# Splitting half of one weight row into a 126-partition and a 2-partition transfer, in a decode kernel that streams 309 MB

## The chip, the core and the metric

The kernel runs on one core of one Trainium2 chip. The metric is the device time of that core in microseconds (us), from one execution of the program; three runs of the kernel before gave 720.33, 720.45 and 720.57 us, median 720.45. The profiled execution was a fourth run of 720.52 us. Its span, from the first to the last profiled instruction, is 718.7 us; the remaining 1.8 us lie around the span.

## The reference

Two branches read the same two tokens `x` (2 x 576) and are mixed by a gate:

```
g = sigmoid(sum(x * gate_w))
q = x @ wq                                   # 32 heads of 128
scores = q . k_cache / sqrt(128)             # k_cache: 2 x 32 x 4096 x 128
a = (softmax(scores) @ v_cache) @ wo         # wo: 4096 x 576
b = gelu(x @ w1 + b1) @ w2 + b2              # w2: 4608 x 576
out = g * a + (1 - g) * b                    # 2 x 1 x 576
```

All of it is float32. Nearly all bytes are the two caches, 128 MiB each; `wq`, `w1`, `w2` and `wo` are 9 to 11 MB each.

## The kernel before, in words

One large SBUF tile, `ring`, has three slots of 64 KiB per partition. Projections come first: `wq` and `w1` are loaded into the ring, q and the hidden layer are computed, and the small inputs (`x`, `gate_w`, `b1`, `b2`) come by ACT's queue. Then 16 passes follow, each with four heads of one batch element: K goes into slots 0 and 1 in turn, V into slot 2. VectorE multiplies K by q (line 521), POOL and VectorE sum over the head dimension (lines 525 to 528), ScalarE takes the exponentials (549), and TensorE multiplies by V (564) and collects into bank 1 (581).

The last stage loads `w2` and `wo` into slots as they come free, on SP's queue. The rows are named by number: `wo` is seen as 128 partitions with 32 rows of 576 columns each, so "row r" of `wo` is a 128 x 576 matrix with one 2304-byte piece in each partition. `w2` has 36 such rows. The transfers stand in this order:

| transfer | rows | bytes per partition | slot |
|---|---|---|---|
| w2 | 0-13, 14-27 | 32256 each | 2 |
| w2 | 28-35 | 18432 | 1 |
| wo | 0-8 | 20736 | 1 |
| wo | 9-15 | 16128 | 1 |
| wo | 16-22 | 16128 | 0 |
| wo | 23-26, 27-29, 30 | 9216, 6912, 2304 | 0 |
| wo | 31 in three parts | 1152, 576, 576 | 0 |

Slot 0 holds the last V until `attend` of the last pass has read it; the transfers into slot 0 therefore wait for TensorE.

TensorE then goes through the rows in the same order: `acc_mm` (line 428) makes two products of 288 columns for each row of `w2` and for rows 0 to 22 of `wo`, into bank 0; rows 23 to 31 go as four products of 144 columns into bank 7 (`part`, line 699). After row 26 the half-sums of bank 0 are folded in (`folds`, 706). Row 31 is taken in the three parts in which it arrives. The result is copied by VectorE and ScalarE (724) and stored by SP (727).

Order and waits are made by a small class, `Flow`. Each `op` names what it reads (`r`), writes (`w`) and shares in writing (`a`); `plan` turns these into semaphore waits, and each transfer has a semaphore of its own (`d1`, `d2`, ...), so that a consumer waits for the whole transfer. Within an engine the order is that of the program's text. `load_rows` (607) issues one transfer for a run of rows and notes for each row where it lies and by which name it is waited for; `row` (648) looks that up for TensorE.

Of the kernel before, what the change touches and what calls it, by code (L numbers as in the profile page):

```python
# [12 lines left out]
P = 128  # L13
# [120 lines left out]
def kernel(  # L134
# [16 lines left out]
    D = x.shape[-1]  # L151
# [20 lines left out]
    DO = D // NC  # L172
# [5 lines left out]
    SLOT = R * DH  # L178
# [14 lines left out]
    ring = rp.tile([P, SLOTS * SLOT], F32, name="ring")  # L193
# [16 lines left out]
    hg = cp.tile([P, NF, B], F32, name="hg")  # L210
# [3 lines left out]
    def temp(n, parts=P):  # L214
        t = ring[:parts, used["t"]:used["t"] + n]
        used["t"] += n
        assert used["t"] <= SLOTS * SLOT
        return t
# [12 lines left out]
    with tc.tile_critical() as section:  # L231
        f = Flow(nc, {"first": first})
# [10 lines left out]
        def pe(fn, r=(), w=(), a=(), loop=None):  # L243
            return f.op("pe", fn, r, w, a, loop=loop)

        def load(out_, in_, r=(), w=(), e="sp", key=None, a=()):
            f.seq = getattr(f, "seq", 0) + 1
            key = key or f"d{f.seq}"
            at = f.at[e]
            return f.op(e, lambda: at.dma_start(out_, in_), r, w, a, dma=key)  # L250
# [3 lines left out]
        def mm(o, lhsT, rhs, start, stop):  # L254
            return ten.matmul(o, lhsT, rhs, start=start, stop=stop, skip_group_check=True)  # L255


        at = 0
        wts = {}
        for name, w in (("wq", wq), ("w1", w1)):  # L260
            n = w.shape[1]
# [22 lines left out]
        for b in range(B):  # L284
# [20 lines left out]
            r=["ident"], w=["pick"],  # L305
# [73 lines left out]
        def gather():  # L379
# [11 lines left out]
            r=["ident"], w=["mine"],  # L391
# [4 lines left out]
            r=["ident"], w=["row4"],  # L396
# [7 lines left out]
        for g in range(N // NQ):  # L404
            u = g * NQ
            t = temp(NQ * DH, NO).rearrange("p (u d) -> p u d", u=NQ)
# [12 lines left out]
                r=[f"bank{b}"], w=[f"q{g}"],  # L419
# [4 lines left out]
        def half_mm(lhsT, rhs, k, s, start=False):  # L424
            o = 64 * (k % 2) + 32 * s
            return mm(acc[o:o + lhsT.shape[-1]], lhsT, rhs, start, False)

        def acc_mm(lhsT, rhs, k, start=False):
            for s in range(NS):
                i = half_mm(lhsT, rhs[:, s * DS:(s + 1) * DS], k, s, start)  # L430
            return i
# [153 lines left out]
        for i in range(N):  # L585
# [10 lines left out]
            s = i % 2  # L596
# [7 lines left out]
        srcs = {"w2": w2.rearrange("(p r) n -> p (r n)", r=NF), "wo": wo.rearrange("(p r) n -> p (r n)", r=32)}  # L604
        rows = {}

        def load_rows(o, w, a, z, part=None):
            lo, hi = part or (a * D, z * D)
            name = f"{w}:{lo}"
            load(ring[:, o:o + hi - lo], srcs[w][:, lo:hi], w=[name], r=[f"free{o // SLOT}"])  # L610
            for r in range(a, z):
                first, end = max(r * D, lo), min((r + 1) * D, hi)
                rows.setdefault((w, r), []).append((first - r * D, end - r * D, o + first - lo, name))
            return o + hi - lo
# [9 lines left out]

        release(2)
        o = load_rows(2 * SLOT, "w2", 0, 14)
        o = load_rows(o, "w2", 14, 28)
        release(1)
        o = load_rows(SLOT, "w2", 28, NF)
        o = load_rows(o, "wo", 0, 9)  # L630
        o = load_rows(o, "wo", 9, 16)
        assert o <= 2 * SLOT
        attend(k, "slot0")
        release(0)
        o = 0
        for a, z in ((16, 23), (23, 27), (27, 30), (30, 31)):
            o = load_rows(o, "wo", a, z)
        for a, z in ((0, DS), (DS, DS + DO), (DS + DO, D)):
            o = load_rows(o, "wo", 31, 32, (31 * D + a, 31 * D + z))
        used["e"] = o  # L640

        def late(n, parts=P):
            t = ring[:parts, used["e"]:used["e"] + n]
            used["e"] += n
            assert used["e"] <= SLOT
            return t

        def row(w, r, lo=0, hi=D):
            for a, z, o, name in rows[w, r]:
                if a <= lo and hi <= z:  # L650
                    return ring[:, o + lo - a:o + hi - a], name

        keep(k)
        combine(k)
# [8 lines left out]
        oP = late(B * 32).rearrange("p (b c) -> p b c", b=B)  # L663
# [7 lines left out]
            r=["bank1", "free0"], w=["osum"],  # L671
# [14 lines left out]
        dve(lambda: vec.tensor_copy(oP.rearrange("p b c -> p (b c)"), opps), r=["bank5"], w=["oP"])  # L686

        for r in range(NF):
            t, name = row("w2", r)
            pe(lambda t=t, r=r: acc_mm(hg[:, r], t, r), r=["hg", name], a=["bank0"])  # L690
        for r in range(FOLD):
            t, name = row("wo", r)
            pe(lambda t=t, r=r: acc_mm(oP[:, :, r], t, r), r=["oP", name], a=["bank0"])

        sums2 = late(DS)
        act(lambda: sca.copy(sums2, acc), r=["bank0", "free0"], w=["sums2"])
        res = bank[7][:32 * (NC - 1) + B, :DO]

        def part(r, s):
            t, name = row("wo", r, s * DO, (s + 1) * DO)  # L700
            pe(
                lambda: mm(res[32 * s:32 * s + B], oP[:, :, r], t, r == FOLD, r == 31),
                r=["oP", name], a=[f"bank7"] if r < 31 else [f"bank7", f"res{s}"],
            )

        def folds():
# [5 lines left out]
        for r in range(FOLD, 31):  # L712
            for s in range(NC):
                part(r, s)
            if r == FOLD + 3:
                pe(folds, r=["fold", "sums2"], a=["bank7"])
        osb = late(D, B)
        for h in ((0, 1), (2,), (3,)):
            for s in h:
                part(31, s)  # L720
            for s in h:
                on, cpy = (dve, vec.tensor_copy) if s % 2 == 0 else (act, sca.copy)
                on(
                    lambda s=s, cpy=cpy: cpy(osb[:, s * DO:(s + 1) * DO], res[32 * s:32 * s + B]),  # L724
                    r=[f"res{s}", "free0"], w=[f"osb{s}"],
                )
# [35 lines left out]
```

## Time and profile before

| what | value |
|---|---|
| runs | 720.33, 720.45, 720.57 us |
| profiled execution | 720.52 us, span 718.7 us |
| moved by DMA | 308.70 MB, mean 430 GB/s |
| VectorE busy | 518.2 us (72%) |
| TensorE matmuls busy | 242.9 us (34%) |
| POOL busy, ScalarE busy | 144.2 us, 41.6 us |
| chain that ended last | DMA 56%, VectorE 38%, TensorE 4% |

The busy share of the 16 DMA engines stands at nine tenths or more in 39 of the 40 slices of the span. In short stretches that share comes out up to a tenth above or below what it is over a long one, and 1.00 is read as all 16 engines at work. A queue row of the page gives packets, not transfers: each partition's contiguous piece is a packet of its own, and completions are counted as packets too.

### The profile page before, as it was taken

Reading aid. Unit: us, or ns where it says so; the run is one execution under the profiler, and the core shown is the slowest. Engines: PE = TensorE matmul, PEld = TensorE weight load, DVE = VectorE, ACT = ScalarE, POOL = GpSimd, SP = SyncE. Lnnn points to the kernel's source line nnn. Section 1 sums busy time; section 2 is a strip of 40 time slices with the busy share of each in tenths; the row PEclk is TensorE's granted clock in tenths of the full one; section 3 lists DMA queues with packets and bytes.
Section 4 is the critical chain, followed back from the end, with each engine's and each line's share of the span. In section 5 each row is a group of like instructions: output and inputs, shape, how many; then the busy total and the mean of one; then the engine's idle time right before and its main releaser. Section 6 shows DMA issues by size and latency. Waiting matters only on the chain.

```text
span 718.7 us, 3902 instructions
## 1 busy us (share of the span) xinstructions
PE 242.9 (34%) x1659; PEld 69.3 (10%) x1659; DVE 518.2 (72%) x150; ACT 41.6 (6%) x157; POOL 144.2 (20%) x28
## 2 busy tenths in 40 slices
PE   0685005141514132140605060514123150506566
PEld 0221001010101000010101010101000010101122
DVE  0103999999969696969698896969696969798100
ACT  0020010101010101010101000010101010101000
POOL 1020133140404040211304040404030220304000
PEclk9977557575656657565657565656656565757888
DMA  9999999999999999999999999999999999999997
GB/s 411 413 420 453 419 456 416 453 419 434 434 427 445 423 452 423 445 423 430 441 427 445 423 452 423 445 423 423 449 423 449 423 449 423 441 427 427 422 429 319
DMA packets 7075, 308.70 MB, mean 430 GB/s; under 512 B 782, under 2 KB 1166, under 8 KB 1436
## 3 DMA queue, kind: packets, MB, share of 16 engines
q1 hardware_dynamic: 7044, 308.55, 99.3%
q8 instruction: 5, 0.08, 0.0%
q10 hardware_dynamic: 24, 0.05, 0.0%
q14 instruction: 2, 0.02, 0.0%
HBM read 308.59 MB, written 0.00 MB: 429 GB/s over the span
## 4 chain that ended last, share of the span: by engine, by line
DMA 56%; DVE 38%; PE 4%; POOL 0%; issue 0%; ACTq 0%; ACT 0%; POOLq 0%; DVEq 0%
DMA ring<-in_A_k_cache_dram 43%; DVE ring L521 22%; DVE st L526 11%; DMA ring<-in_A_v_cache_dram 6%; DVE st L528 5%; DMA ring<-in_A_wo_dram 4%; PE bank L255 4%; DMA ring<-in_gate_w_dram 3%; POOL ring L275 0%; PE bank L320 0%; DVE mxt L597 0%; DVE bs L538 0%; ACTq L250 0%; POOL ring L369 0%; DVE ring L313 0%
## 5 line engine op out<-in xcount | busy, mean ns | idle before, releaser
L521 DVE TENSOR_TENSOR ring<-ring,q_all 128x16384 f32<-128x16384 f32 x16 | 275.6, 17224 | 84.4 <-DMA ring<-in_A_k_cache_dram 84.4
L255 PE MATMUL bank<-ring,p_all 128*32 128x512 f32 x1024 | 148.4, 744 | 342.7 <-DMA ring<-in_A_v_cache_dram 342.7
L525 POOL TENSOR_TENSOR ring<-ring 128x3968 f32<-128x3968 f32 x16 | 137.9, 8622 | 473.1 <-DVE ring L521 473.1
L526 DVE TENSOR_REDUCE st<-ring 128x66 f32<-128x8448 f32 x16 | 143.2, 8953 | 0.5
L255 PEld LDWEIGHTS bank<-ring,p_all 128*32 128x32 f32 x1024 | 36.1, 133 | 460.4 <-DMA ring<-in_A_v_cache_dram 355.5
L528 DVE TENSOR_REDUCE st<-ring 128x62 f32<-128x3968 f32 x16 | 68.6, 4286 | 0.6
L549 ACT ACTIVATE p_all<-st,bs 32x128 f32<-32x128 f32 x64 | 25.5, 398 | 561.1 <-DVE bs L538 560.5
L255 PE MATMUL bank<-ring 128*32 128x384 f32 (+8 forms) x410 | 49.0, 538 | 10.7 <-DMA ring<-in_A_wo_dram 7.0
L255 PE MATMUL bank<-ident,mxt 128*128 128x128 f32 x32 | 9.6, 390 | 90.9 <-DVE mxt L597 90.9
L491 DVE TENSOR_TENSOR ring<-bank,ring 128x384 f32<-128x384 f32 x3 | 1.5, 553 | 33.3 <-PE bank L255 33.3
L255 PE MATMUL bank<-avs,now 128*64 128x512 f32 x32 | 24.1, 844 | 2.0 <-DVE avs L574 0.9
L724 DVE COPY ring<-bank 2x144 f32<-2x144 f32 x2 | 0.6, 300 | 32.7 <-PE bank L255 32.7
L574 DVE TENSOR_TENSOR avs<-bank,selr 128x512 f32<-128x512 f32 x16 | 10.9, 680 | 16.0 <-PE bank L255 16.0
L255 PEld LDWEIGHTS bank<-ring 128*32 128x32 f32 (+5 forms) x410 | 18.4, 124 | 40.7 <-issue 23.4
L255 PEld LDWEIGHTS bank<-ident,mxt 128*128 128x128 f32 x32 | 5.9, 232 | 105.2 <-DVE mxt L597 105.2
L313 DVE COPY ring<-ring 3x64 f32<-3x64 f32 x2 | 0.3, 183 | 19.1 <-DMA ring<-in_gate_w_dram 19.1
L549 ACT ACTIVATION_READ_ACCUMULATOR p_all<-st,bs 32x1 f32 x64 | 11.8, 184 | 0.0
L255 PE MATMUL bank<-ring,hg 128*2 128x288 f32 x144 | 11.0, 461 | 2.3 <-DMA ring<-in_B_w_dram 2.3
L408 POOL TENSOR_TENSOR ring<-ring 64x512 f32<-64x512 f32 x4 | 4.0, 1038 | 37.8 <-ACT ring L386 37.8
L320 PE MATMUL bank<-ident,ring 3*128 3x3 f32 x6 | 0.9, 254 | 23.6 <-DVE ring L313 23.6
L538 DVE TENSOR_REDUCE bs<-bank 128x4 f32<-128x128 f32 x16 | 4.7, 291 | 2.3 <-PE bank L255 2.3
L597 DVE TENSOR_REDUCE mxt<-st 128x1 f32<-128x128 f32 x16 | 4.6, 286 | 0.6
(65 smaller groups left out, 33.4 us busy)
## 6 DMA issues: line engine op xcount, KB each, us to landing
ring<-in_B_w_dram SPq DMA_DIRECT2D x1, 9216.0 KB, 46.5
ring<-in_B_w_dram SPq DMA_DIRECT2D x2, 4032.0 KB, 23.2
ring<-in_A_wo_dram SPq DMA_DIRECT2D x2, 2016.0 KB, 37.0
ring<-in_A_wo_dram SPq DMA_DIRECT2D x1, 2592.0 KB, 38.5
ring<-in_B_w_dram SPq DMA_DIRECT2D x1, 2304.0 KB, 32.9
ring<-in_B_w_dram SPq DMA_DIRECT2D x1, 1152.0 KB, 48.8
ring<-in_A_wo_dram SPq DMA_DIRECT2D x1, 1152.0 KB, 33.6
ring<-in_A_wq_dram SPq DMA_DIRECT2D x1, 1024.0 KB, 24.0
```

The costliest lines, as they stand in the source:

```text
L255: return ten.matmul(o, lhsT, rhs, start=start, stop=stop, skip_group_check=True)
L320: i = ten.transpose(xps[:, c, :B + 1], s, ident[:B + 1, :B + 1])
L408: lambda t=t, u=u: gps.tensor_mul(t, qall.unsqueeze(1).to_broadcast([NO, NQ, DH]), mine[:, u:u + NQ].unsqueeze(2).to_broadcast([NO, NQ, DH ...
L491: lambda m=m, b=b: vec.tensor_add(hrow[:, m * FC:(m + 1) * FC], bank[b][:, :FC], b1r[:, m * FC:(m + 1) * FC]), r=[f"bank{b}", "b1r"], a=[" ...
L521: lambda: vec.tensor_mul(kt, kt, q.unsqueeze(1).to_broadcast([P, R, DH])),
L525: pool(lambda: gps.tensor_add(h[:, :, :DH2], h[:, :, :DH2], h[:, :, DH2:]), r=[name], a=[name + "h"])
L526: dve(lambda: vec.tensor_reduce(st[s][:, HALVED:], kt[:, HALVED:], AX.X, ALU.add), r=[name], w=[f"st{s}"])
L528: lambda: vec.tensor_reduce(st[s][:, :HALVED], h[:, :, :DH2], AX.X, ALU.add),
L538: lambda: vec.tensor_reduce(bs[s], mt.rearrange("o (e p) -> o e p", e=E), AX.X, ALU.max, negate=True),
L549: ins = sca.activation(p[w, :, e * RB:(e + 1) * RB], st[s][w].rearrange("p (t c) -> p t c", c=RB), AF.Exp, bias=bs[s][w, e:e + 1], accum_o ...
L574: lambda: vec.tensor_mul(avs, av.rearrange("p (r d) -> p r d", d=DH), selr.unsqueeze(2).to_broadcast([P, RB, DH])), r=["bank4", "selr"], w ...
L597: dve(lambda s=s: vec.tensor_reduce(mxt, st[s], AX.X, ALU.max), r=[f"st{s}"], w=["mxt"])
```

## The change

The transfer of `wo`'s rows 9 to 15 stops 288 columns earlier, in the middle of row 15. The last 288 columns of row 15 (1152 bytes in each partition) come after it in two transfers: partitions 0 to 125, then partitions 126 and 127. They lie in the ring where they lay before. `load_rows` gets `cuts`, the partitions at which a piece is divided, and shares the name among the parts (`a` in place of `w`); `row` now returns all names that a row needs, and TensorE waits for all of them. Nothing else is computed or moved.

```diff
-        def load_rows(o, w, a, z, part=None):
+        def load_rows(o, w, a, z, part=None, cuts=()):
             lo, hi = part or (a * D, z * D)
             name = f"{w}:{lo}"
-            load(ring[:, o:o + hi - lo], srcs[w][:, lo:hi], w=[name], r=[f"free{o // SLOT}"])
+            edges = (0, *cuts, P)
+            for p0, p1 in zip(edges, edges[1:]):
+                load(ring[p0:p1, o:o + hi - lo], srcs[w][p0:p1, lo:hi], a=[name], r=[f"free{o // SLOT}"])
...
-        o = load_rows(o, "wo", 9, 16)
+
+        pieces = ((288, (126,)),)
+        at = 16 * D - sum(n for n, _ in pieces)
+        o = load_rows(o, "wo", 9, 16, part=(9 * D, at))
+        for n, cuts in pieces:
+            o = load_rows(o, "wo", 15, 16, part=(at, at + n), cuts=cuts)
+            at += n
...
         def row(w, r, lo=0, hi=D):
-            for a, z, o, name in rows[w, r]:
-                if a <= lo and hi <= z:
-                    return ring[:, o + lo - a:o + hi - a], name
+            parts = [p for p in rows[w, r] if p[0] < hi and lo < p[1]]
+            (o,) = {o - a for a, _, o, _ in parts}
+            return ring[:, o + lo:o + hi], [name for _, _, _, name in parts]
...
         for r in range(FOLD):
-            t, name = row("wo", r)
-            pe(lambda t=t, r=r: acc_mm(oP[:, :, r], t, r), r=["oP", name], a=["bank0"])
+            t, names = row("wo", r)
+            pe(lambda t=t, r=r: acc_mm(oP[:, :, r], t, r), r=["oP", *names], a=["bank0"])
```

On SP's queue, in the last stage (`in_B_w_dram` is here `w2`, `in_A_wo_dram` is `wo`, the shapes are partitions x float32 columns, and `s_pe` is TensorE's semaphore):

```order
 L250 DMA ring<-in_B_w_dram 128x4608 [waits s_dve]
 L250 DMA ring<-in_A_wo_dram 128x5184
-L250 DMA ring<-in_A_wo_dram 128x4032
+L250 DMA ring<-in_A_wo_dram 128x3744
+L250 DMA ring<-in_A_wo_dram 126x288
+L250 DMA ring<-in_A_wo_dram 2x288
 L250 DMA ring<-in_A_wo_dram 128x4032 [waits s_pe]
 L250 DMA ring<-in_A_wo_dram 128x2304
```

Two transfers are added ahead of the one that waits for TensorE; nothing is moved past another.

On TensorE, at `wo`'s rows 9 to 22 (bank_69 is bank 0; `s_d47` is the transfer of rows 9 on, before and now, `s_d48` before and `s_d50` now that of rows 16 to 22, and `s_d48` and `s_d49` now the parts of 126 and 2 partitions):

```order
 L255 MATMUL bank_69<-ring 2x288 [waits s_d47]
+L255 MATMUL bank_69<-ring 2x288 x11
+L255 MATMUL bank_69<-ring 2x288 [waits s_d49,s_d48]
+L255 MATMUL bank_69<-ring 2x288
+L255 MATMUL bank_69<-ring 2x288 [waits s_d50]
 L255 MATMUL bank_69<-ring 2x288 x13
-L255 MATMUL bank_69<-ring 2x288 [waits s_d48]
-L255 MATMUL bank_69<-ring 2x288 x13
```

The 14 products of rows 9 to 15 stay as they were; the last two of them now wait for the two new transfers.

More of the change, by code (lines that the diff above doesn't have):

```diff
@@ L688 @@
         for r in range(NF):
-            t, name = row("w2", r)
-            pe(lambda t=t, r=r: acc_mm(hg[:, r], t, r), r=["hg", name], a=["bank0"])
+            t, names = row("w2", r)
+            pe(lambda t=t, r=r: acc_mm(hg[:, r], t, r), r=["hg", *names], a=["bank0"])
         for r in range(FOLD):
-            t, name = row("wo", r)
-            pe(lambda t=t, r=r: acc_mm(oP[:, :, r], t, r), r=["oP", name], a=["bank0"])
+            t, names = row("wo", r)
+            pe(lambda t=t, r=r: acc_mm(oP[:, :, r], t, r), r=["oP", *names], a=["bank0"])
         sums2 = late(DS)
@@ L699, in part @@
         def part(r, s):
-            t, name = row("wo", r, s * DO, (s + 1) * DO)
+            t, names = row("wo", r, s * DO, (s + 1) * DO)
             pe(
                 lambda: mm(res[32 * s:32 * s + B], oP[:, :, r], t, r == FOLD, r == 31),
-                r=["oP", name], a=[f"bank7"] if r < 31 else [f"bank7", f"res{s}"],
+                r=["oP", *names], a=[f"bank7"] if r < 31 else [f"bank7", f"res{s}"],
             )
```

## The prediction

> **What bounds the kernel now.** I read the page's queue part first, then the end of the chain of waits, then short stretches of the last microseconds.
>
> ```profile
> DMA packets 7075, 308.70 MB, mean 430 GB/s; under 512 B 782, under 2 KB 1166, under 8 KB 1436
> q1 hardware_dynamic: 7044, 308.55, 99.3%
> q8 instruction: 5, 0.08, 0.0%
> q10 hardware_dynamic: 24, 0.05, 0.0%
> q14 instruction: 2, 0.02, 0.0%
> ```
>
> SP's queue (q1) fills the 16 DMA engines for 99.3% of the span, so the kernel is a stream of bytes with a short tail. The change moves the same bytes. It can only act on the tail, or on how evenly the 16 engines end. The chain of waits from 660 us on:
>
> ```profile
> 669.41 8.90 PE bank L255 x64
> 678.32 0.02 issue
> 678.33 31.21 DMA ring<-in_A_wo_dram
> 709.54 0.04 issue
> 709.58 6.76 PE bank L255 x108
> 716.35 0.02 issue
> 716.37 0.27 ACT ring L724
> ```
>
> After rows 16 to 22 of wo have landed at 709.54, the chain is put down to TensorE for 6.76 us. The timeline shows whether that is so to the end:
>
> ```profile
> 704.82 2.11 PE L255 MATMUL bank<-ring 128*2 128x288 f32 x28 [0.48 <-DMA ring<-in_A_wo_dram]
> 709.58 4.77 PE L255 MATMUL bank<-ring 128*2 128x288 f32 x60 [2.65 <-DMA ring<-in_A_wo_dram]
> 714.43 1.90 PE L255 MATMUL bank<-ring 128*2 128x144 f32 x40
> 715.48 0.53 PEld L255 LDWEIGHTS bank<-ring 128*2 128x2 f32 x8 [0.21 <-DMA ring<-in_A_wo_dram]
> ```
>
> Row 31's first part finds the weight load idle for 0.21 us, waiting for a transfer. So TensorE has caught up by 715.48, and the last three transfers end the kernel, with TensorE at most about 0.2 us behind them. An earlier landing can win no more than that, and a later one costs its whole delay.
>
> How do the 16 engines reach that end? The share of DMA times 16 is the number of engines still at work (columns: stretch, its length, busy time of PE, PEld, DVE, ACT and POOL, granted clock, DMA share, GB/s):
>
> ```profile
> 700.00:710.00 10.00, 6.81 (x72) 2.27 (x76) 0.00 (x0) 0.00 (x0) 0.00 (x0) 0.83 0.99 421
> 712.80:713.20 0.40, 0.40 (x14) 0.38 (x8) 0.00 (x0) 0.26 (x1) 0.00 (x0) 0.50 1.03 412
> 713.50:714.00 0.50, 0.50 (x15) 0.45 (x9) 0.00 (x0) 0.00 (x0) 0.00 (x0) 0.50 0.86 305
> 714.60:715.00 0.40, 0.40 (x20) 0.34 (x16) 0.00 (x0) 0.00 (x0) 0.00 (x0) 1.00 0.43 147
> 715.00:715.20 0.20, 0.20 (x16) 0.11 (x12) 0.00 (x0) 0.00 (x0) 0.00 (x0) 1.00 0.43 135
> 715.20:715.40 0.20, 0.20 (x16) 0.07 (x7) 0.00 (x0) 0.00 (x0) 0.00 (x0) 1.00 0.32 95
> 715.40:715.50 0.10, 0.10 (x10) 0.02 (x4) 0.00 (x0) 0.00 (x0) 0.00 (x0) 1.00 0.19 58
> 715.50:715.55 0.05, 0.05 (x6) 0.05 (x4) 0.00 (x0) 0.00 (x0) 0.00 (x0) 1.00 0.06 12
> 715.55:715.60 0.05, 0.05 (x6) 0.03 (x4) 0.00 (x0) 0.00 (x0) 0.00 (x0) 1.00 0.00 0
> ```
>
> All 16 are at work at 713.2; from 714.6 to 715.2 it is 0.43 x 16 = 7; then 0.32 x 16 = 5; in 715.40 to 715.50 it is 0.19 x 16 = 3; the last is done at 715.55. So nine engines finish about a microsecond early, and seven engines, spread over the last half microsecond, decide the end. Seven is also the number of instruction packets on q8 and q14 (5 + 2). That these seven made seven engines late is my inference; the page does not name engines.
>
> **How a transfer is divided.** The packet counts tell. On q1, 48 loads of 128 partitions, one of them with two pieces per partition, make 6272 data packets, and the store has 2. That leaves 7044 - 6274 = 770 = 48 x 16 + 2, so a 128-row load has one completion on each of 16 engines, 8 rows each, and the 2-row store uses two engines. On q10 two loads of 4 rows and four of one row make 12 data packets and leave 12 completions, as 4 + 4 + 4 x 1 would. Rows are thus shared out in equal counts. For 126 rows the largest equal sharing is 14 engines with 9 rows; no row shows this number of rows, so 2 engines with 63 rows and an uneven 16 stay as bounds.
>
> [...]
>
> **The change part by part.** *What the engines carry.* Over 700 to 710 us an engine moves 421 / (0.99 x 16) = 26.6 bytes per ns. The large transfer loses 8 rows x 1152 = 9216 bytes on each engine: -0.35 us. Fourteen engines get 9 x 1152 = 10368 bytes back, in short packets. At 26.6 bytes per ns that takes 0.39 us; at the rate of the shortest packets in the trace, 147 / (0.43 x 16) = 21.4, it takes 0.48; in 712.8 to 713.2, where rows of 6912, 2304 and 1152 bytes are mixed, it is 412 / (1.03 x 16) = 25.0 and 0.41. I take the last as the nearest row. Net: +0.07 us (bounds +0.04 and +0.14), and with one completion more, +0.08. [...] Two engines are relieved by 0.35 us.
>
> *What that does to the end.* The end is the latest of the seven. If no relieved engine is the last, it moves by +0.08 (bounds +0.04 and +0.19, the last if the engine with ten rows is last and packets cost most). If both relieved engines are the very last two, the third, done about 0.05 before the end, takes over: 0.08 - 0.05 = +0.03, and with the lowest price about 0. Five late engines remain in any case, three of them busy until 715.40 or later at most. So there is hardly anything to win: I take +0.08.
>
> *Writing to other partitions.* [...] Whether two engines then meet at one place in SBUF is not shown. Below, nothing; above, the short rows run at half speed, +0.4 us. I take nothing, since it concerns 0.4 us of work while the others are at large rows, and keep the bound.
>
> *TensorE.* Rows 9 to 14 and half of row 15 land 0.35 us sooner. TensorE begins them at 704.82 after waiting 0.48, so they start up to 0.35 sooner; row 15 then waits for its two parts, which land at about the old time plus 0.08. It costs nothing: after these 28 instructions (2.11 us) TensorE idles 2.65 us until rows 16 to 22. Without that cover row 15's two products would cost their 0.08 us of delay. Those rows and all later ones land 0.08 later, which is the term already counted, since TensorE's 709.58 follows that landing.
>
> *SP's queue.* Two more transfers are issued, ahead of the one that waits for TensorE at 678.33:
>
> ```profile
> 660.11 1.40 SPq L250 DMA_DIRECT2D ring<-in_B_w_dram  x3
> 661.55 29.35 SPq L250 DMA_DIRECT2D ring<-in_A_wo_dram  x9
> L250 SPq DMA_DIRECT2D ring<-in_A_wo_dram x9: 328/432/5517, 661.6 to 686.2; - x9
> DMA to landing us min/median/max: 29.7/35.2/42.7
> ```
>
> An issue takes 0.43 us by the median: 0.9 us, in the stretch of more than ten microseconds in which SP waits for TensorE's last reading of V (669.41 to 678.31). The last issues take up to 5.5 us, as if SP were held until earlier transfers complete. Two more in front may hold the rest for two more such spells, 11 us. The shortest way from issue to landing is 29.7 us, so data are still queued ahead of them. If that cover were gone, the engines would idle for what is missing; it takes over 18 us more.
>
> *Sum.* +0.08 us on the profiled 720.52, or 720.60. That execution lies 0.07 us above the median of the runs, so the median becomes 720.53.
>
> **The rivals.** *The relieved engines are the late ones.* For: some two of 16 are relieved and seven of 16 are late. Against: five others are as late within 0.3 us. It gives 0 to +0.03, 720.45 to 720.5. [...]
>
> *The 126 rows go to two engines.* For: 126 is odd times two, and a sharing by powers of two fits 16, 4, 2 and 1 as well. Each would carry 63 x 1152 = 72.6 KB, 2.7 us at 26.6 and 3.4 at 21.4 bytes per ns. If the two are among the seven late ones, the end moves by that less the 0.35 taken away, +2.4 to +3.0; if they are among the nine that end 1 to 2 us before, by +0.4 to +2.0. It costs from the point where the extra work exceeds their lead. Together 720.9 to 723.5, middle 722.2: slower.
>
> *An instruction packet falls on another engine.* The five on q8 are 16 KB each: 0.6 us of one engine. Should the two longer instruction streams (three more issues on SP, two more waits on TensorE) move one onto an engine that is late already, the end moves by +0.6: 721.1. For: seven late engines suggest that every such packet leaves a mark. Against: the added instructions are few.
>
> *TensorE's clock.* The granted clock changes in steps:
>
> ```profile
> 703.79:710.62 6.83, 3.70 (x55) 1.22 (x52) 0.00 (x0) 0.00 (x0) 0.00 (x0) 1.00 0.98 416
> 710.62:714.03 3.41, 3.41 (x46) 1.90 (x42) 0.00 (x0) 0.40 (x1) 0.00 (x0) 0.50 0.97 391
> 714.03:716.40 2.37, 2.30 (x58) 1.20 (x48) 0.44 (x2) 0.30 (x2) 0.00 (x0) 1.00 0.28 95
> ```
>
> If TensorE's earlier start on rows 9 to 14 shifted the halved step onto 714.03, the 1.3 us of products from there to 715.4 would take twice that, and the end would move by about +1.0: 721.5. Against: the work and its place change by 0.35 us in a stretch of 6.83.
>
> **How the numbers follow.** Chances: the forecast 0.70; relieved engines last 0.09; instruction packet 0.07; clock 0.05; half-speed short rows (+0.4, 720.85) 0.04; two engines 0.05. The likeliest gives 720.53. The runs before differ by 0.24 us, so I put the low end at 720.3; the instruction packet's 721.1 and most of what lies below sets the high end, 721.1. That leaves out the clock, the two engines and strays. About 0.2% (1.44 us) is what a measurement of this kernel can tell from no change. Only two engines (0.04 of its 0.05) and two mishaps at once (0.02) go beyond it: slower 0.06. For faster no mechanism is found, since TensorE is 0.2 us behind at most: 0.02. Same: 0.92.
>
> **What would show it.** SP's queue should count 7044 + 126 + 14 + 2 + 2 = 7188 packets with fourteen engines, 7176 with two, 7190 with sixteen. The DMA share in the last microsecond should still be above 0.3, for five engines or more, and fall to zero within 0.2 us of where it did against the landing of rows 16 to 22; TensorE's idle time before rows 16 to 22 should grow from 2.65 to about 3.0 us. A time below 720.2 would mean that the two relieved engines alone set the end, and one above 721.9 that the short parts are not shared as I think.

## The result, and the profile after

The changed kernel took 721.18 us (median of 22 runs, 720.83 to 722.20), the kernel before 720.47 us in runs beside it (22 runs, 720.16 to 720.60): +0.71 us, ratio 1.0013 with a 95% interval of 1.0007 to 1.0019. It is slower by 0.10%, half of what I had called the limit of telling, but clear of noise: the lowest of its 22 runs lies above the highest of the kernel before. The time lies 0.08 us above the range that I gave. Here and below, differences are those of the medians; the ratios are not formed from the medians and can differ a little from these. Where an experiment below has runs of 758 us and more, they are listed one by one: the comparison sets runs more than 1.5% above a kernel's fastest aside, and its ratio does not contain them.

The profiled execution took 722.1 us, span 720.3, and is one of the slower of the 22. A second profile of the same kernel, in the first experiment, took 720.97 us, span 719.2, and stands for the usual run. In the page of the first, the queue part reads:

```profile
DMA packets 7219, 308.70 MB, mean 429 GB/s; under 512 B 798, under 2 KB 1310, under 8 KB 1580
q1 hardware_dynamic: 7188, 308.55, 99.3%
q8 instruction: 5, 0.08, 0.0%
```

7188 packets, 144 more than before (128 rows and 16 completions), are what I had counted for 14 engines with nine rows each and two with one. The experiment with a spare transfer below shows the 14 by themselves: behind the uncut columns, whose count is 7188 as well, a transfer of 126 rows makes it 7328, which is 126 rows and 14 completions more, and one of 128 rows makes it 7332, 128 and 16 more. With one completion for each engine, the rows go to as many engines as I thought; which partitions each engine gets, no count tells. The end of the chain of waits is another than before:

```profile
680.11 35.84 DMA ring<-in_A_wo_dram
715.95 0.04 issue
715.99 1.90 PE bank L255 x40
717.89 0.02 issue
717.91 0.28 ACT ring L732
```

Before, the chain went over to TensorE at 709.54, when rows 16 to 22 had landed. Now it stays with the transfers until rows 27 to 29 have landed at 715.95. TensorE's rows show the same, in the timeline of the usual run:

```profile
710.07 2.11 PE L255 MATMUL bank<-ring 128*2 128x288 f32 x28 [2.86 <-DMA ring<-in_A_wo_dram]
712.81 1.17 PE L255 MATMUL bank<-ring 128*2 128x144 f32 x32 [0.63 <-DMA ring<-in_A_wo_dram]
714.88 1.90 PE L255 MATMUL bank<-ring 128*2 128x144 f32 x40 [0.65 <-DMA ring<-in_A_wo_dram]
```

TensorE waits for a transfer before each group shown, so nothing on TensorE makes the end late. The transfers do. Short stretches show where; the columns are those of the prediction's tables, and the last two, DMA share and GB/s, are what counts. First the kernel before:

```profile
702.50:705.50 3.00, 2.52 (x28) 0.77 (x24) 0.00 (x0) 0.00 (x0) 0.00 (x0) 0.78 1.00 430
706.00:712.00 6.00, 3.35 (x40) 1.01 (x32) 0.00 (x0) 0.00 (x0) 0.00 (x0) 0.89 0.97 408
```

Then the changed kernel in its usual run:

```profile
702.50:705.50 3.00, 2.98 (x24) 0.67 (x20) 0.00 (x0) 0.00 (x0) 0.00 (x0) 0.52 1.05 379
706.00:712.00 6.00, 3.14 (x46) 1.00 (x36) 0.00 (x0) 0.00 (x0) 0.00 (x0) 1.00 0.98 411
```

And in the execution of 722.1 us:

```profile
702.50:705.50 3.00, 3.00 (x24) 0.67 (x20) 0.00 (x0) 0.00 (x0) 0.00 (x0) 0.53 1.05 365
706.00:712.00 6.00, 2.59 (x42) 0.91 (x38) 0.00 (x0) 0.00 (x0) 0.00 (x0) 1.00 0.99 394
```

GB/s divided by 16 times the share is what an engine at work moves in a ns. Around the 126-partition transfer that falls from 430 / 16.0 = 26.9 bytes to 379 / 16.8 = 22.6 and 365 / 16.8 = 21.7. All engines are busy and move about a sixth less. What isn't moved in the three microseconds is (430 - 379) x 3 = 153 KB, 0.36 us at 430 GB/s, in the usual run, which took 0.45 us more than the profiled execution before, and 195 KB, 0.45 us, in the other.

A lower mean could still come from slow short rows alone, which is the bound that I had given. The trace keeps the time of every packet, that is of each partition's piece of a transfer, and decides it. These are the packets that start between 704 and 705 us:

| packets of | kernel before | changed kernel, usual run |
|---|---|---|
| 16128 bytes | 601 ns each (30 packets) | 720 ns on average, from 618 to 808 (22 packets) |
| 1152 bytes | none | 59 ns on average (25 packets) |

Undisturbed, a packet of 1152 bytes takes 51 ns, as in the experiment with uncut columns below. The short packets lose 8 ns each; the large ones, which belong to the next transfer, lose 119 ns each, and none of them is as fast as before. The loss is theirs. After 706 us the usual run is back at 411 / 15.7 = 26.2 bytes, as before (408 / 15.5 = 26.3); the execution of 722.1 us stays at 394 / 15.8 = 24.9. There are thus two slow stretches: one at the cut in both profiles of it, and a longer one that follows it in one of the two.

### The profile page after: what moved, and what is told of

It reads as the page before. It is cut to its first block, busy times and chain, and to the rows that moved or that the text cites. A ratio compares the mean times of both kernels' runs of the same rounds, so it can differ in the third digit from the quotient of the medians.

```text
span 720.3 us, 3905 instructions
## 1 busy us (share of the span) xinstructions
PE 240.3 (33%) x1659; PEld 68.3 (9%) x1659; DVE 518.3 (72%) x150; ACT 41.6 (6%) x157; POOL 144.2 (20%) x28
## 3 DMA queue, kind: packets, MB, share of 16 engines
q1 hardware_dynamic: 7188, 308.55, 99.3%
## 4 chain that ended last, share of the span: by engine, by line
DMA 57%; DVE 38%; PE 4%; POOL 0%; issue 0%; SPq 0%; ACTq 0%; ACT 0%; POOLq 0%; DVEq 0%
DMA ring<-in_A_k_cache_dram 43%; DVE ring L521 22%; DVE st L526 11%; DMA ring<-in_A_v_cache_dram 6%; DVE st L528 5%; DMA ring<-in_A_wo_dram 5%; PE bank L255 4%; DMA ring<-in_gate_w_dram 3%; POOL ring L275 0%; PE bank L320 0%; SPq L250 0%; DVE mxt L597 0%; DVE bs L538 0%; ACTq L250 0%; POOL ring L369 0%
## 5 line engine op out<-in xcount | busy, mean ns | idle before, releaser
L549 ACT ACTIVATE p_all<-st,bs 32x128 f32<-32x128 f32 x64 | 25.5, 398 | 563.6 <-DVE bs L538 563.0
L255 PE MATMUL bank<-ring 128*32 128x384 f32 (+8 forms) x410 | 45.7, 517 | 12.8 <-DMA ring<-in_A_wo_dram 9.0
L255 PE MATMUL bank<-avs,now 128*64 128x512 f32 x32 | 24.3, 851 | 1.9 <-DVE avs L574 0.9
L255 PEld LDWEIGHTS bank<-ring 128*32 128x32 f32 (+5 forms) x410 | 17.1, 118 | 41.0 <-issue 21.5
## 6 DMA issues: line engine op xcount, KB each, us to landing
ring<-in_B_w_dram SPq DMA_DIRECT2D x2, 4032.0 KB, 24.3
```

The costliest lines, as they stand in the source:

```text
L549: ins = sca.activation(p[w, :, e * RB:(e + 1) * RB], st[s][w].rearrange("p (t c) -> p t c", c=RB), AF.Exp, bias=bs[s][w, e:e + 1], accum_o ...
```

## The experiments

Each experiment changes the changed kernel; the times stand against runs of the kernel before on the same chip, taken beside it. In the code, `...` marks what is left out. "Bytes per ns" is, as above, GB/s over 16 times the share in 702.5 to 705.5 us.

**The changed kernel again.** No edit.

> The changed kernel once more. In the first profile of it the packets of all 16 DMA engines took about 1.25 times their usual time from 703.0 to 705.7 us, right at and behind the 126-partition transfer (+0.6 us), and about 1.1 times from 707.8 to 714.7 (+0.6 us). Theory 1, shares of nine rows crowd the writes into SBUF: the first slow stretch is always there, the second need not be, and the median is +0.5 to +0.8 us over the kernel before. Theory 2, the slow stretches are chance of that one execution: neither shows again and the median is within 0.2 us of before.

721.08 against 720.50 us, +0.58, ratio 1.0011 (1.0002 to 1.0020); 9 of 11 runs lie between 720.94 and 721.25 and two at 721.84 and 721.89. Its rows stand above: the first slow stretch is there, the second is not. The loss isn't chance. The two longer runs fit the second stretch, but no profile shows them.

**The same columns, uncut.**

```diff
-        pieces = ((288, (126,)),)
+        pieces = ((288, ()),)
```

> The 288 columns come by themselves but in one transfer of 128 partitions. Theory 1 (crowding by shares that are not the usual eight rows): no slow stretch, time within +0.2 us of before. Theory 3 (one more short transfer in the queue is enough, by its short rows or by its place between large ones): slow stretch and +0.5 us as with the changed kernel.

720.56 against 720.50 us, +0.06, ratio 1.0001 (0.9992 to 1.0010).

```profile
702.50:705.50 3.00, 3.00 (x28) 0.99 (x24) 0.00 (x0) 0.00 (x0) 0.00 (x0) 0.50 1.07 450
```

450 / 17.1 = 26.3 bytes per ns: no slow stretch. Every packet of 16128 bytes that starts from 702 to 708 us takes 601 ns again. One more transfer of 128 partitions, its short rows and its place in the queue cost next to nothing (theory 3 falls); cutting it does. TensorE's clock stands at 0.50 in this stretch, as in the changed kernel, so the clock isn't the cause either.

**Cut at 112, and at 120.**

```diff
-        pieces = ((288, (126,)),)
+        pieces = ((288, (112,)),)
```

(and `(120,)` in the second kernel)

> Cut at 112: shares of seven rows on 16 engines and then one row on each of 16. No engine is relieved. Theory 1 (shares that are not the usual eight rows): slow stretch as with 126, +0.4 to +0.8 us. Theory 4 (what harms is that two engines get ahead of the others, or that 14 carry more): no slow stretch, within +0.2 us of before.

> Cut at 120: shares of eight rows on 15 engines, then one row on each of eight engines; the sixteenth gets nothing. Theory 1, if an engine's share is the same eight neighbouring partitions as in a 128-partition transfer: only the eight single rows are out of place, slow stretch absent or under 0.2 us. Theory 4 (uneven engines): slow stretch, +0.3 us or more.

721.01 us, +0.51, with 112, ratio 1.0007 (0.9998 to 1.0016); 721.11 us, +0.61, with 120, ratio 1.0009 (1.0000 to 1.0018). By the first interval alone 112 could be no change, but its lowest run, 720.83 us, lies above 32 of the 33 runs of the kernel before. The two rows, 112 first:

```profile
702.50:705.50 3.00, 2.34 (x24) 0.61 (x20) 0.00 (x0) 0.00 (x0) 0.00 (x0) 0.76 1.06 389
```

```profile
702.50:705.50 3.00, 2.11 (x24) 0.46 (x20) 0.00 (x0) 0.00 (x0) 0.00 (x0) 0.71 1.08 376
```

22.9 and 21.8 bytes per ns: both slow. If 112 rows are shared out equally, as 120, 126 and 128 rows are by their completions (15, 14 and 16), all 16 engines carry seven rows and then one, and theory 4 (uneven engines) falls for this stretch. With 120 q1 counts 7195 packets, 151 more than the kernel before: 128 rows and 23 completions, as 15 shares of eight rows and 8 single rows give; whether the sixteenth engine has one of these, the count does not tell. Eight rows are a share as in a whole transfer, and it is slow all the same: either my condition, that eight neighbouring rows are an engine's usual share, does not hold, or theory 1 does not. No trace here names partitions.

**Two halves, eight sixteenths, and twice the width.**

```diff
-        pieces = ((288, (126,)),)
+        pieces = ((288, (64,)),)
```

(`tuple(range(16, P, 16))` for the cuts in the second kernel; `((576, (126,)),)` in the third)

> Two transfers of 64 partitions, four rows on each of 16 engines in both. No engine is relieved or loaded more. Theory 1 (an engine that writes to other partitions than in a 128-partition transfer crowds the engine that writes there): half of the engines write into the other half's partitions, slow stretch as with 126 or longer, +0.3 to +0.9 us. Theory 4 (uneven engines): none, within +0.2.

> Eight transfers of 16 partitions, one row on each of 16 engines in each. Theory 1: all 16 engines write into 16 neighbouring partitions at a time, the worst crowd that these bytes allow, so more than with 126: +0.8 to +2 us. Theory 5 (any unusual sharing costs one fixed disturbance, whatever the place): +0.5 us as with 126, 120 and 112, plus up to 0.05 for seven more completions.

> The cut at 126 on all 576 columns of row 15: the same shares, twice the bytes. Theory 1: crowding lasts about twice as long, +0.9 to +1.3 us. Theory 5 (fixed disturbance): +0.5 to +0.7 us.

With halves 721.24 us, +0.72 (ratio 1.0011, 1.0002 to 1.0020); with sixteenths 721.39, +0.87 (1.0014, 1.0005 to 1.0023); with twice the width 722.62, +2.10 (1.0025, 1.0015 to 1.0035), nine runs between 721.55 and 723.51. In that order:

```profile
702.50:705.50 3.00, 0.52 (x8) 0.20 (x12) 0.00 (x0) 0.00 (x0) 0.00 (x0) 0.86 1.05 359
```

```profile
702.50:705.50 3.00, 2.41 (x30) 0.75 (x26) 0.00 (x0) 0.00 (x0) 0.00 (x0) 0.85 1.07 375
706.00:712.00 6.00, 2.60 (x28) 0.68 (x24) 0.00 (x0) 0.00 (x0) 0.00 (x0) 0.85 0.96 404
```

```profile
702.50:705.50 3.00, 2.85 (x24) 0.67 (x20) 0.00 (x0) 0.00 (x0) 0.00 (x0) 0.50 1.09 300
706.00:712.00 6.00, 1.64 (x28) 0.48 (x24) 0.00 (x0) 0.00 (x0) 0.00 (x0) 1.00 0.98 355
```

21.4, 21.9 and 17.2 bytes per ns. Even halves, which by equal sharing change no engine's load, cost as much as 126 + 2. Sixteenths cost little more, and more than theory 5 allowed: inside what theory 1 allowed, but at its lower end, so the loss does not grow with the crowd as I had reckoned. Twice the bytes cost 3.0 to 3.6 times as much, more than either theory said. The rows show why, as far as the profiled execution goes, which with 723.51 us is the slowest of the nine: the first stretch is deeper, and it does not recover after 706: 355 / 15.7 = 22.6 bytes per ns, against 26.3 in the kernel with sixteenths (404 / 15.4). It is the longer slow stretch again, and with more bytes it seems to come more often.

**The two rows alone.** The columns uncut, then partitions 126 and 127 once more into free columns; this adds 2.3 KB of loads whose values are not used, though row 15 waits for them.

```diff
-        pieces = ((288, (126,)),)
+        pieces = ((288, ()),)
...
+        load(ring[126:, o:o + 288], srcs["wo"][126:, at - 288:at], w=["spare"], r=["free1"])
...
```

> The 288 columns come in one transfer of 128 partitions, and after it the rows of partitions 126 and 127 come a second time, into free columns that nothing uses; row 15 waits for them as well. It is the small transfer alone. Theory 1: two rows are out of place, no slow stretch, within +0.2 us. Theory 6 (the short remainder on few engines is what harms): slow stretch and +0.4 us or more.

720.53 against 720.52 us, +0.01, ratio 1.0001 (0.9992 to 1.0010).

```profile
702.50:705.50 3.00, 2.82 (x36) 0.94 (x32) 0.00 (x0) 0.00 (x0) 0.00 (x0) 0.85 1.09 457
```

457 / 17.4 = 26.2 bytes per ns. The small remainder is harmless; theory 6 falls.

**A spare transfer from another place.** The columns uncut, then 126, or 128, rows of 288 columns from a nearly dense block of K into free columns; row 15 waits for them, the values are not used. The edit for 126 rows:

```diff
...
+        load(ring[:126, o:o + 288], k_cache[0, 0, :378].rearrange("(p r) d -> p (r d)", p=126)[:, :288], w=["spare"], r=["free1"])
...
```

> Row 15's columns come in one transfer of 128 partitions. Behind it a spare transfer of 126 partitions x 288 columns is read from a nearly dense block of K and written to free columns that nothing uses (row 15 waits for it). Its bytes alone cost 145 KB at 430 GB/s, +0.34 us. Theory 1 (the place of writing): slow stretch, +0.8 to +1.4 us over before, 0.4 or more over the next run. Theory 7 (the pattern in which wo's rows are read from HBM): no slow stretch, +0.3 to +0.5 us.

> The same spare transfer with 128 partitions, the comparison for the one before. Both theories: its bytes alone, +0.3 to +0.5 us, no slow stretch.

With 126 rows 721.50 us, +0.98 (ratio 1.0015, 1.0005 to 1.0024); with 128 rows 720.92, +0.40 (1.0006, 0.9997 to 1.0015). In that order:

```profile
702.50:705.50 3.00, 2.39 (x27) 0.63 (x23) 0.00 (x0) 0.00 (x0) 0.00 (x0) 0.78 1.06 356
```

```profile
702.50:705.50 3.00, 2.64 (x40) 0.95 (x34) 0.00 (x0) 0.00 (x0) 0.00 (x0) 0.95 1.05 429
```

21.0 against 25.5 bytes per ns, and 0.58 us more for two rows fewer. With 128 rows the time is that of the bytes, 0.34 us by the expectation, and little else. The pattern in which wo is read is not needed for the loss (theory 7 falls). What the runs show is that transfers of 16, 64, 112, 120 or 126 rows slow the rows around them, and transfers of 128 or of two rows don't. That it is the sharing, with other rows on each engine than in a transfer of 128, would fit all of them, but no trace shows which engine takes which row. If engines get in each other's way, whether at the writing or elsewhere is not told by these runs, since a new sharing would move both ends of a transfer.

**The cut at the end.** Rows 9 to 15 as before the change; the last transfer of all, 144 columns of row 31, is cut at 126.

```diff
...
-            o = load_rows(o, "wo", 31, 32, (31 * D + a, 31 * D + z))
+            o = load_rows(o, "wo", 31, 32, (31 * D + a, 31 * D + z), (126,) if z == D else ())
...
```

> Rows 9 to 15 as before the change; the very last transfer, 144 columns of row 31, is cut at 126 instead. No large transfer comes behind it. Theory 1: little time for crowding, half the bytes and only late engines left: -0.05 to +0.25 us. Theory 5 (fixed disturbance): +0.4 to +0.6 us.

720.51 against 720.52 us, -0.01, ratio 1.0000 (0.9991 to 1.0009). Where nothing follows in the queue this cut, of half the columns, costs nothing, and theory 5 (a fixed disturbance) falls. It agrees with the packet times: what is lost is lost by the neighbours, whose large rows run beside and behind the cut. Nor does the relief of two engines win anything here, where it comes last.

**The cut earlier.** Rows 9 to 15 of wo as before the change; the last 288 columns of w2's rows 14 to 27 are cut, at 126 and then at 64.

```diff
-        o = load_rows(o, "w2", 14, 28)
+        at = 28 * D - 288
+        o = load_rows(o, "w2", 14, 28, part=(14 * D, at))
+        o = load_rows(o, "w2", 27, 28, part=(at, 28 * D), cuts=(126,))
...
```

> Rows 9 to 15 of wo as before the change; the last 288 columns of w2's rows 14 to 27 come by themselves, cut at 126: the same shares some 16 us earlier, from another matrix. Theory 1: the slow stretch moves to about 686 to 689 us, and since the engines have no idle time to make it up, +0.4 to +0.7 us at the end. Theory 7: none or a different size. If the time is within 0.2 us although the stretch is there, a loss that early is made up later.

> The cut in w2's rows 14 to 27 as in the earlier run, but into two halves of 64 partitions, so that all engines carry the same. Theory 4b (the lasting slow stream needs engines that are shifted against each other by uneven shares): all 11 runs within +0.4 to +1.0 us. Otherwise some runs at +2 us or more, as the 3 of 11 with the cut at 126.

At 126: 721.20 us, +0.68 (ratio 1.0019, 1.0009 to 1.0030), of 11 runs seven between 720.86 and 721.25, one at 721.91 and three between 723.63 and 723.78. At 64: 721.20 us, +0.67 (1.0010, 1.0001 to 1.0018), all runs between 720.99 and 721.41. The stretch 684 to 690 us, first of the kernel before, then of the cut at 126:

```profile
684.00:690.00 6.00, 5.84 (x76) 2.15 (x72) 0.00 (x0) 0.00 (x0) 0.00 (x0) 0.77 1.01 435
```

```profile
684.00:690.00 6.00, 4.80 (x84) 1.90 (x80) 0.03 (x1) 0.00 (x0) 0.00 (x0) 1.00 0.94 366
```

26.9 against 24.3 bytes per ns. The stretch moved with the cut, to another matrix, and nothing was made up in the 26 us that follow. The three runs at +3.2 us would fit a stream that stays a tenth slow for those 26 us (2.6 us, and the 0.6 of the others); none of them was profiled. At 64 no run was that long, as theory 4b forecast.

**The cut in the middle of the K stream.** wo as before the change; the ninth K tile comes with its last 288 columns by themselves, cut at 126, at 64, and uncut.

```diff
...
+            if i == 8:
+                to, of, c = slot(i % 2), heads(k_cache, i), SLOT - 288
+                for lo, hi, p0, p1 in ((0, c, 0, P), (c, SLOT, 0, 126), (c, SLOT, 126, P)):
+                    load(to[p0:p1, lo:hi], of[p0:p1, lo:hi], a=[f"slot{i % 2}"])
+                return
...
```

> wo's rows as before the change; the last 288 columns of the ninth K tile come by themselves, cut at 126, in the middle of the stream of 64 KB rows. Theory 8 (the slowed stream lasts as long as the engines work without a break): most runs at +0.4 to +0.8 us, and some runs, about a quarter, at +5 to +30 us. Theory 9 (it belongs to the short rows of w2 and wo): all runs within +0.4 to +0.9 us. If the K stream has room to make up the loss: within +0.2.

> As the cut in the ninth K tile, but into two halves of 64 partitions: crowding as before, all engines carry the same. Theory 4b (the lasting slow stream needs uneven shares): all runs within +0.3 to +1.0 us. Otherwise about half of the runs or more at +30 us and above.

> The last 288 columns of the ninth K tile by themselves in one transfer of 128 partitions. Both theories: no crowding, all runs within +0.2 us of before. A run above +1 us would mean that a separate short transfer is enough for the lasting slow stream.

| cut | runs | times, us |
|---|---|---|
| at 126 | 6 | 720.97 twice; 759.10, 763.45, 763.75, 769.00 |
| at 64 | 12 | nine from 720.99 to 721.28; 758.40, 761.58, 769.14 |
| uncut | 11 | 720.33 to 720.74 (+0.12, ratio 1.0001, 0.9992 to 1.0010) |
| kernel before | 40 beside these and the cut of w2 at 64 | 720.27 to 720.85 |

With the cut, the quiet runs lose 0.44 to 0.82 us, about as at the end of the program. In the profile of one of them (cut at 126), packets of 65536 bytes that start from 358 to 360 us take 2767 ns on average, 2418 before, and 2419 from 362 to 370 us: the short slow stretch is there, and it passes. But seven of 18 runs lose 38 to 49 us. When the cut comes is told by the kernel before, in whose chain of waits the ninth K tile lands at 313.49 + 46.68 = 360.2 us:

```profile
313.49 46.68 DMA ring<-in_A_k_cache_dram
```

Some 356 us of loads are left then, to 716; 38 to 49 us are 11 to 14% of these. From 706 to 712 us the profiled execution of 723.51 us above moved 1 - 22.6 / 26.3 = 14% less, and the one of 722.1 us 5%. Theory 8, that what began at the cut lasts as long as the loads run without a break, would thus fit, but I had expected a quarter of the runs at +5 to +30 us, and at 126 it was four of six at +38 and more. No profile caught a long run, so neither the cause of these runs nor what their engines did is shown. Theory 4b has the three long runs of 12 with even halves against it. Uncut, none was seen in 11 runs.

## Why the prediction was right or wrong

The forecast was 720.53 us, no change that a measurement could tell, with a range of 720.3 to 721.1; measured were 721.18. The step that failed is "Writing to other partitions". I had a disturbance of this kind there, with a bound of +0.4 us, took nothing for it, and gave it a chance of 0.04 because it concerned only 0.4 us of work "while the others are at large rows". That reason was the error. The others at large rows are those who pay: their packets take 720 ns in place of 601 at the cut, and the engines together lose a sixth of their speed for some three microseconds. The packets of the short rows, which by the bound would run at half speed, take 59 ns in place of 51. That half speed had no row behind it, so it is luck that its +0.4 us comes near. The cut at the end shows the same from the other side: with nothing behind it, it costs -0.01 us. The right size of the term was about +0.5 us: the medians of the cuts at 126, 120 and 112 are +0.58, +0.61 and +0.51, with the same columns uncut +0.06. Of the 22 runs 16 have their median at 721.1, +0.6 us; the other six lie between 721.86 and 722.20. One of these is the profiled execution with the longer slow stretch, which I hadn't thought of; whether the other five have it too is not shown. Why the large rows are slowed, at the writing to SBUF or elsewhere, stays open.

The rest by its steps:

- *How the rows are divided*: right in the number of engines. 7188 packets, as forecast for 14 engines and 2; the spare transfer of 126 rows has 14 completions.
- *The bytes of the engines, +0.08 us, and no gain from relieving two of seven*: not contradicted, too small to be seen by itself. By the packet times it was a little more: nine short packets at 51 ns are 0.46 us, while eight large ones that shrink from 601 to 559 ns give back 0.34, so about +0.13 with the completion (9 ns), inside the bounds. The tenth row that the upper bound, +0.19, puts on an engine is shown by no run: no trace tells which engines take the two rows. In its place, the two rows alone cost +0.01 us. The cut at 112, which by equal sharing relieves nobody, costs 0.51, the one at 126 costs 0.58. In the usual run the engines still at work half a microsecond before the last row lands are 0.43 x 16 = 7, as many as before:

```profile
715.20:715.40 0.20, 0.20 (x16) 0.17 (x12) 0.00 (x0) 0.00 (x0) 0.00 (x0) 1.00 0.43 138
```

- *TensorE*: right in its place. It idles 2.86 us before rows 16 to 22 instead of 2.65; I had said 3.0. The last row lands 5.9 us after rows 16 to 22, against 6.0 before, as forecast. Row 15's delay was hidden in that idle time, as forecast. But TensorE, 0.2 us behind before, is now ahead at every later landing and has nothing to hide the rest with.
- *SP's queue*: right. The issue that was held longest took 9.2 us instead of 5.5, and the shortest way from issue to landing fell from 29.7 to 20.1 us, which still covers it. In the usual run the transfers' group reads:

```profile
L250 SPq DMA_DIRECT2D ring<-in_A_wo_dram x11: 235/433/9193, 661.5 to 696.3; - x11
DMA to landing us min/median/max: 20.1/34.9/42.9
```

- *The rivals*: two engines for 126 rows is refuted by those 14 completions. In the usual run TensorE's clock stands at 1.00 in 706 to 712 us (0.89 before) and at 0.52 in 702.5 to 705.5 (0.78 before): the halved step came before 705.5 us, not at the end, and TensorE waits behind it anyway. An instruction packet on another engine is not needed to explain anything; q8 still has five. In the profile before each of the five took 0.88 to 1.03 us, more than the 0.6 that I had reckoned. The change adds two issues to SP's stream, not the three that I named there.
- *Within 0.2%*: right, +0.10%, but not for the reason given: the largest term was the one that I had taken as nothing.

## What to carry to other kernels

In a full stream like this one, keep a load at 128 partitions. Cutting 147 KB of it into 126 + 2, 120 + 8, 112 + 16, 64 + 64 or eight times 16 cost 0.5 to 0.9 us, and the same bytes as one transfer of their own cost next to nothing (+0.06). Other kernels were not tried. When a bound concerns a shared resource, price it on everybody who uses that resource at the time, not on the instruction that is added; and before relieving the latest of 16 engines, count how many are as late as the last, for here there were seven.

## What the runs showed that I had not expected

A short cut can leave the stream slow long after it has passed. In one profile (twice the width, 723.51 us) an engine moves 22.6 bytes per ns for microseconds after the cut, with all transfers whole again, in place of 26.3. The packet times show how even this is and when it ends: packets of 16128 bytes that start from 706 to 708 us all take 719 to 734 ns, 601 before; packets of 6912 bytes still take 306 ns on average from 713 to 716 us, 262 before; from 717 us on the short packets that are left take their usual time again (in the kernel before 51 ns for 1152 bytes, 29 for 576). In the execution of 722.1 us the second stretch is weaker: 289 ns for the 6912-byte packets from 713 to 715 us, 262 for the three that start later.

With 288 columns cut in the middle of 309 MB, 7 of 18 runs took 758 to 769 us instead of 721; the kernel before, in 159 runs of this study, never took more than 720.92. Whether the same slow stream, kept up for longer, makes these runs is not shown. What keeps the engines slow, and why only in some executions, is open. A shift of the engines against each other, or writes that stay piled up, are two guesses of mine, and no run here shows either.
